# Softmax sums of couples 7 to 9 put in front of the next scores, in a fused attention and SiLU kernel on one core

## The chip, the cores and the metric

The kernel runs on one core of one Trainium2 chip. The metric is device time in microseconds (us) of one execution; the number that counts is the median of the runs. All data is float32 inside; inputs arrive as float64 where the reference makes them so (the weights `w_in` and `w_out`) and are rounded on the chip.

## The reference, cut to what matters

There are 8 batches of 12 heads, 448 rows and a head width of 64; the model width is 768, the hidden width 2048.

```python
q_n, k_n = rmsnorm(q, g_q), rmsnorm(k, g_k)          # each (8, 12, 448, 64)
scores = (1 / sqrt(64)) * q_n @ k_n.T
attn = exp(scores - max);  attn = attn / (sum(attn) + 1e-9)
x = (attn @ v) -> rows (8*448, 12*64)
h = x @ w_in                                          # (3584, 2048)
out = (h * sigmoid(h)) @ w_out                        # (3584, 768)
```

## The kernel before, in words

**Couples.** Four heads of one batch are a couple (two pairs of two heads). There are NC = 24 couples; GROUP = 6 couples make two batches, LATE is 9 and SOON is 11. The attention of the couples and the first matrix product (x @ w_in) of the two batches before run interleaved on TensorE: couple c is one `visit(c)` (scores, exponentials on ScalarE, weighted sums of v) followed by one `between(c)` in which TensorE is filled with products of x @ w_in. In the trace a visit of couple 8 or later begins with the two small matmuls of line 718 (the row factors of a later couple) and the first scores of line 752.

**The first product.** It is computed by a seven-product scheme in blocks m = 0 to 7 (`Seven`): the products are called "1" to "7" and run in the order 1, 2, 6, 5, 7, 3, 4. Each takes three matmuls of 128x448, recorded as six, into a PSUM bank of its own. The results of 1 and 5 are copied out by ScalarE (L974, L983), those of 2, 6, 7, 3 and 4 are added on VectorE (L912, `plus`); POOL adds two more terms from SBUF (L984, L987). Before "3" is taken out, POOL's L984 has to be done, and before "4", L987.

**PSUM banks.** Products take their bank alternately from two pools: `mm` with two buffers, and, in stretches, `sc` with two buffers, which the scores use as well. A buffer is free for its next user when the instruction that empties it is done. So in `mm` each product waits until the one two places earlier in `mm` has been taken out.

**Softmax sums.** `sum_up(c)` adds the exponentials over the keys by four matmuls with a block of ones (L832, tiles of 128x32, recorded as eight). Then VectorE takes reciprocals in two halves (L841), copies them (L847), and four small DMAs on SyncE's queue spread them over partitions (`spread`, L850). `divide` (L863) multiplies the weighted sums with them. For an ordinary couple L832 stands within the second half of `between(c)`, in a bank of `sc`, and `divide` reads the weighted sums of v from their PSUM banks in the next visit, with one operand in PSUM and one in SBUF. For couples in the list `LAGGED` (before: 10, 12 to 16, 18 to 22) L832 stands at the very end of `between(c)`, just in front of the next couple's scores, in a bank of `mm`; the two reciprocals run in the next visit (`lagging`), the weighted sums are copied to SBUF without division, and `divide` runs on SBUF data within the next `between`.

**Rounding w_in.** The 24 pieces of `w_in` are each loaded ahead by SyncE (L88), opened by two ScalarE instructions (L103, L104, step "o") and rounded by three VectorE instructions (L126, L129, L133) and one of POOL (L137, step "r"). `halves` says which steps run in which half of which `between` (two halves for each couple from GROUP on: entry 0 is couple 6's first half, entry 3 couple 7's second, 5 couple 8's second, 7 couple 9's second); `visits` says which run in a visit. A round issues the next load. `sum_w_in(i, step)` makes the four sums of chunk i of six pieces that products 6, 5, 7 and 3 use (steps 1, 0, 2 and 3; VectorE on 128x768, L912 and L909).

**The order of work.** The kernel writes the order out by hand: a piece of VectorE, ScalarE, POOL or SyncE work is emitted between matmuls at fixed shares of a `fill`, and each engine runs its queue in that order. Nothing is reordered at run time.

**Other lines named below.** L475 and L474 sum and square k rows; L503 and L722 raise to the power -1/2 on POOL; L731 scales q rows; L682 and L686 transpose q and k on VectorE, L692 applies the gains on ScalarE; L803 adds exponentials; L699 and L705 square and sum q; L643 and L674 are TensorE's transposes of earlier couples; L314, L325, L327, L255, L287 and L289 load v, q and k; L1002 saves hidden rows.

Of the kernel before, what the change touches and what calls it, by code (L numbers as in the profile page):

```python
# [542 lines left out]
def bounded(  # L543
# [10 lines left out]
    NC, loads, place, norm, spare, ones, first, squares = (  # L554
        own[name] for name in ("NC", "loads", "place", "norm", "spare", "ones", "first", "squares")
    )
    GROUP, LATE = z.NPAIR, z.LATE
    EARLY = GROUP - 1
    SOON = 2 * GROUP - 1
    FULL = (GROUP, SOON - 1)  # L560
    LAGGED = [c for c in range(SOON - 1, NC) if c % GROUP != GROUP - 1]


    hidden = dram.tile([z.NF, P, z.B * S], F32, name="hidden")
# [6 lines left out]
    work = mem.tile([P, 16 * S + z.NK], F32, name="work")  # L571
# [11 lines left out]
    r = [piece(S) for _ in range(2)]  # L583
# [10 lines left out]
    late = [extra[:, ds(2 * z.NW * S - (i + 1) * n, n)].bitcast(I32) for i in range(2)]  # L594
# [71 lines left out]
    def transpose_k(c):  # L666


        assert z.KB == BANK
        t = ps.tile([P, 2, BANK], F32, name="sc", bufs=2)  # L670
        rows = place[f"k{c % 2}"]
        for i in range(2):
            for j in range(z.KEYS + 1 - i):
                nc.tensor.transpose(t[:, i, ts(j, P)], rows[:, ds((z.KA, z.KB)[i] + j * P, P)], ident)  # L674
        columns = t.rearrange("p i s -> p (i s)")[:, 0 : z.NK]
        nc.scalar.activation(kT, columns, AF.Copy, scale=gains)
        loads["k" if c < LATE - 1 else "quarters"](min(c + 2, LATE))

    def flip(c, name):

        if name == "q":
            nc.vector.transpose(qT.rearrange("p i s -> p (i s)"), q_of(c)[:, 0 : z.NK])  # L682
            if c > SOON:
                load_q(c + 1)
            return
        nc.vector.transpose(kT, place[z.BY_QUARTERS])  # L686
        if c + 1 < NC:
            loads["quarters"](c + 1)
# [171 lines left out]
    def divide(c, source):  # L860
        for i in range(2):
            x = x_of(c, i)
            nc.vector.tensor_tensor(  # L863
                out=x, in0=x if source is None else source[i], in1=factors(c)[i], op=ALU.mult
            )
# [155 lines left out]
    def sum_w_in(i, step):  # L1021

        assert room.w_in.rounded >= (i + 1) * z.NW
        summed.add((i, step))
        w = room.chunk(i).rearrange("p (c m r k) -> p c m r k", c=z.NW, m=2, r=2)
        up, low = w[:, 0:HW], w[:, HW:]
        s = room.sums(i).rearrange("p (s c m k) -> p s c m k", s=3, c=HW, m=2)
        left_sums(
            up[:, :, :, 0], low[:, :, :, 0], up[:, :, :, 1], low[:, :, :, 1],
            s[:, 0], s[:, 1], s[:, 2], (step,),  # L1030
        )
# [165 lines left out]
    for at in ((1, 2), (2, 1), (2, 2)):  # L1197
        a = take(2 * z.HALF)
        results[at] = [a[:, ts(t, z.HALF)] for t in range(2)]
    a = take(2 * z.HALF)  # L1200
# [251 lines left out]


    step_of = {"o": lambda: room.w_in.open(), "r": lambda: room.w_in.round()}
    halves = {0: "ro", 1: "ro", 2: "ro", 3: "oro", 4: "or", 5: "oor", 6: "o", 7: "oroo"}
    visits = {GROUP + 2: "rr", GROUP + 3: "r", GROUP + 4: "rr"}
    for c in range(GROUP // 2):
        halves[2 * (c - GROUP)], halves[2 * (c - GROUP) + 1] = "rr", "o"
    halves[-2], halves[-1] = "r", ""
# [3 lines left out]
    sums_visits = {GROUP + 1: 1, GROUP + 3: 2}  # L1463
# [4 lines left out]
        return work + [lambda a=a: sum_w_in(*a) for a in sums_halves.get(i, ())]  # L1468

    def weights_in_visit(c):  # L1470
        for step in visits.get(c, "")[1:]:
            step_of[step]()
        rows = [lambda: scale_rows(c + 1, nc.vector)] if LATE - 1 <= c < SOON else []
        if c in sums_visits:
            sum_w_in(sums_visits[c], 0)
        run_all(rows)
        if c in sums_visits:
            for step in range(1, 4):
                sum_w_in(sums_visits[c], step)

    def last_two(c):
# [2 lines left out]
    def visit(c):  # L1484

        beside = normalise(c + 1) if 0 < c <= GROUP else []
        if c == GROUP:
            beside = [lambda: None] + beside[2:]
        if c < NC:
            scores(c, 0, 0)  # L1490
        for step in visits.get(c, "")[:1]:
            step_of[step]()
        if lagging:
            lagging.pop(0)()
        if c == 0:
            first_q(1)
            normalise_alone(1)
            scores(c, 1, 0)
        if c == 0:
            run_all(beside[0:1])  # L1500
        else:
            weigh(c - 1, LEFT)
            weigh(c - 1, LEFT - 1, 0)
            turn(1, nc.scalar.copy if c <= GROUP else nc.vector.tensor_copy)
            run_all(beside[0:1])
            if GROUP < c < NC and c % GROUP == 0:
                sum_x(last_two(c), 0, range(2, 4))
        if c < NC:
            scores(c, 0, 1)
        if c > 0:  # L1510
            weigh(c - 1, LEFT - 1, 1)
            if c - 1 < EARLY:
                for i in range(2):
                    nc.vector.tensor_copy(x_of(c - 1, i), sums[i])  # L1514
                run_all(beside[1:2])
                if c == GROUP // 2 + 1:
                    divide(c - 2, None)
                if inverting:
                    while len(inverting) > 1:
                        inverting.pop(0)()  # L1520
                    if c > 1:
                        divide(c - 2, None)
            else:
                if lagging:
                    for i in range(2):
                        nc.vector.tensor_copy(x_of(c - 1, i), sums[i])
                    lagging.pop(0)()
                else:
                    divide(c - 1, sums)
                if c == GROUP:  # L1530
                    for i in range(1, HW):
                        sum_x(last_two(c), i, range(2))
                    for i in range(2):
                        norm.scale(c + 1, q_of(c + 1), q_of(c + 1), i, nc.vector)
                    room.w_in.round()
                run_all(beside[1:2])
                if GROUP < c < NC and c % GROUP == 0:
                    for i in range(1, HW):
                        sum_x(last_two(c), i)
                weights_in_visit(c)  # L1540
            if c + 1 < NC:
                loads["vrest"](c + 1)
        if c == NC:
            return
        if c > 0:
            scores(c, 1, 0)
        scores(c, 1, 1)
        if c <= GROUP:
            run_all(beside[2:3])
        weigh(c, 0, 1)  # L1550
        scores(c, 2, 0)
        weigh(c, 1, 1)
        turn(0, nc.scalar.copy)
        if c < GROUP:
            run_all(beside[3:4])
        scores(c, 2, 1)
        weigh(c, 0, 0)
        if c < GROUP:
            scores(c, LEFT)
        if c != GROUP - 1:  # L1560
            run_all(add(c, 1))
        weigh(c, 1, 0)
        if c < GROUP // 2:
            room.w_in.open()
        if c >= GROUP:
            scores(c, LEFT)
        if c + 1 < NC:
            loads["v"](c + 1)
        if len(inverting) == 1:
            inverting.pop()()  # L1570
# [5 lines left out]
    def between(c):  # L1576

        def transposes_and_sums():
            if c in LAGGED:
                first = [lambda: divide(c - 1, None)] if c - 1 in LAGGED else [lambda: None]  # L1580
                return first + [lambda: None, lambda: flip(c + 1, "k"), gain]
            summing = sum_up(c)
            if c < GROUP - 1:
                transpose_k(c + 1)
            if c < GROUP:
                next(summing)
            if c == GROUP - 1:
                reciprocals = next(summing)
                divide(c - 1, None)
                sum_x([0, 1], 0)  # L1590
                run_all(reciprocals)
                return
            if GROUP <= c < LATE - 1:
                transpose_k(c + 1)
            reciprocals = next(summing)
            if LATE - 1 <= c < NC - 1:
                reciprocals += [lambda: flip(c + 1, "k"), gain]
            if GROUP // 2 < c < EARLY:
                divide(c - 1, None)
            return reciprocals  # L1600
# [23 lines left out]
        late = add(c, LEFT - 1) if c >= GROUP else []  # L1624
# [4 lines left out]
        if c == GROUP:  # L1629
            third, fourth = (  # L1630
                [lambda i=i, step=step: sum_x(last_two(c), i, (step,)) for i in range(1, HW)]
                for step in (2, 3)
            )
            late = third + late + fourth
        late += further[2:] if c >= GROUP else further[:2]
        if c - 1 in LAGGED and c not in LAGGED:
            late.append(lambda: divide(c - 1, None))
# [284 lines left out]
```

## Time and profile before

| | us |
|---|---|
| median of 3 runs | 1294.24 |
| lowest and highest | 1294.24 and 1294.8 |
| profiled execution | 1296.34 |
| its span, first to last instruction | 1294.6 |
| TensorE busy in the span | 1283.5 |
| VectorE busy | 971.4 |
| ScalarE busy | 504.3 |
| POOL busy | 363.5 |

The profiled execution is one run by itself, with 1.74 us outside its span, and stands 2.1 us above the median. The granted TensorE clock is 0.999 over the span. All starts in the lines of the trace are microseconds from the span's start; a line gives start, length, engine, source line, operation, output and inputs, and how many instructions were merged; a bracket tells idle time ahead of it and what ended it. Lengths of successive instructions overlap by some 0.05 to 0.1 us, so queues are best summed from start to start.

In this trace the visits of couples 7, 8, 9, 10 and 11 begin at 147.09, 180.44, 212.35, 244.27 and 276.77 us.

### The profile page before, as it was taken

How to read it: one execution, taken by the hardware profiler on the slowest of the kernel's cores; microseconds unless marked ns; L12 is line 12 of the kernel's file. 1: busy time of each engine (PE TensorE's matmuls, PEld its weight loads, DVE VectorE, ACT ScalarE, POOL GpSimd, SP SyncE). 2: the span in 40 equal slices, each digit the busy share in tenths (PEclk: the TensorE clock that was granted, in tenths of full speed). 3: DMA queues.
4: the chain of work that ended last, by engine and by line, in shares of the span. 5: the costliest groups of instructions: out<-in, count | busy, mean ns of one | idle time of the engine just before them, and what ended most of it. 6: DMA issues, size and time to landing. Idle time of an engine off the chain costs nothing.

```text
span 1294.6 us, 19931 instructions
## 1 busy us (share of the span) xinstructions
PE 1283.5 (99%) x7212; PEld 840.7 (65%) x7212; DVE 971.4 (75%) x1672; ACT 504.3 (39%) x880; POOL 363.5 (28%) x221
## 2 busy tenths in 40 slices
PE   9999999999999999999999999999999999999998
PEld 4444454444444454444544555559999999999998
DVE  6898878868666558666555886798978787878785
ACT  7967666645555554554543344310001000000000
POOL 6765454543344344343311344400000000000000
PEclk9999999999999999999999999999999999999999
DMA  9675347434444444444411466312332313141411
GB/s 232 174 193 136 104 124 197 95 83 102 112 94 91 119 91 102 108 93 93 107 50 69 149 204 219 117 66 88 100 94 86 113 67 129 51 133 48 141 39 40
DMA packets 266160, 144.15 MB, mean 111 GB/s; under 512 B 203748, under 2 KB 249956, under 8 KB 266052
## 3 DMA queue, kind: packets, MB, share of 16 engines
q1 hardware_dynamic: 265424, 141.68, 39.8%
q8 instruction: 59, 0.97, 0.3%
q0 software_dynamic: 320, 0.90, 0.2%
q14 instruction: 49, 0.40, 0.1%
q10 hardware_dynamic: 308, 0.20, 0.1%
HBM read 95.36 MB, written 41.29 MB: 106 GB/s over the span
## 4 chain that ended last, share of the span: by engine, by line
PE 97%; DVE 1%; POOL 1%; issue 0%; ACT 0%; DMA 0%; SPq 0%; ACTq 0%; DVEq 0%; POOLq 0%
PE alone L1285 23%; PE mm L963 21%; PE sc L963 11%; PE av L789 10%; PE sc L752 10%; PE mm L1285 8%; PE alone L963 7%; PE alone L1323 2%; PE mm L832 2%; PE mm L1323 1%; PE sc L643 1%; PE sc L832 1%; PE sc L674 0%; DVE work L912 0%; POOL rms L503 0%
## 5 line engine op out<-in xcount | busy, mean ns | idle before, releaser
L757 ACT ACTIVATE work<-sc,rms 128x448 f32<-128x448 f32 x318 | 182.0, 635 | 98.0 <-PE sc L752 85.7
L752 PE MATMUL sc<-work 64*64 64x448 f32 x1344 | 169.4, 543 | 1.0 <-ACT work L653 0.6
L789 PE MATMUL av<-work,rows 64*64 64x448 f32 x1272 | 155.5, 540 | 1.2 <-DVE x L1514 0.9
L963 PE MATMUL mm<-x,W 128*128 128x448 f32 x366 | 149.1, 542 | 0.0
L963 PE MATMUL mm<-sums_x,W 128*128 128x448 f32 x348 | 142.4, 542 | 0.0
L803 DVE TENSOR_TENSOR work<-work 128x896 f32<-128x896 f32 (+1 forms) x110 | 118.3, 1105 | 28.6 <-PE av L789 28.1
L530 POOL DMA_DIRECT2D out_dram<-x x2 | 1.2, 592 | 443.5 <-DVE x L912 443.5
L503 POOL TENSOR_TENSOR rms<-rms,minus_half 128x14 f32<-128x14 f32 (+4 forms) x40 | 97.4, 2437 | 86.8 <-DVE rms L499 83.3
L963 PEld LDWEIGHTS mm<-x,W 128*128 128x128 f32 x366 | 68.5, 190 | 70.3 <-issue 64.8
L1285 PE MATMUL alone<-W,rows 128*128 128x192 f32 x610 | 113.0, 326 | 0.0
L963 PEld LDWEIGHTS mm<-sums_x,W 128*128 128x128 f32 x348 | 65.1, 190 | 68.1 <-issue 62.5
L789 PEld LDWEIGHTS av<-work,rows 64*64 64x64 f32 x1272 | 65.9, 132 | 62.8 <-issue 19.3
L752 PEld LDWEIGHTS sc<-work 64*64 64x64 f32 x1344 | 60.4, 132 | 63.3 <-ACT work L757 25.3
L1285 PEld LDWEIGHTS alone<-W,rows 128*128 128x128 f32 x610 | 101.4, 190 | 0.0
L963 PE MATMUL sc<-x,W 128*128 128x448 f32 x246 | 99.6, 541 | 0.0
L984 POOL TENSOR_TENSOR stage<-parts,stage 128x448 f32<-128x448 f32 x31 | 39.8, 1285 | 169.2 <-ACT stage L983 168.9
L722 POOL TENSOR_TENSOR rms<-rms,minus_half 128x28 f32<-128x28 f32 x15 | 72.6, 4842 | 48.9 <-DVE rms L719 47.8
L963 PEld LDWEIGHTS sc<-x,W 128*128 128x128 f32 x246 | 46.4, 190 | 47.0 <-issue 46.7
L1285 PE MATMUL alone<-W,work 128*128 128x192 f32 x382 | 72.2, 326 | 0.0
L1295 ACT COPY rows<-alone 128x192 f32<-128x192 f32 x33 | 10.5, 318 | 141.5 <-PE alone L1285 136.7
L1285 PEld LDWEIGHTS alone<-W,work 128*128 128x128 f32 x382 | 63.8, 190 | 0.0
L1116 ACT ACTIVATE stage<-stage 128x896 f32<-128x896 f32 x63 | 56.8, 945 | 17.1 <-DVE stage L912 16.9
(267 smaller groups left out, 2312.8 us busy)
## 6 DMA issues: line engine op xcount, KB each, us to landing
hidden<-stage SPq DMA_DIRECT2D x63, 448.0 KB, 2.9
work<-hidden SPq DMA_DIRECT2D x21, 1024.0 KB, 5.1
rows<-in_moe_w_out_dram SPq DMA_DIRECT2D x32, 384.0 KB, 3.7
W<-in_moe_w_in_dram SPq DMA_DIRECT2D x22, 512.0 KB, 5.3
x<-hidden SPq DMA_DIRECT2D x7, 1024.0 KB, 6.1
rows<-in_q_dram SPq DMA_DIRECT2D x120, 56.0 KB, 2.2
rows<-in_k_dram SPq DMA_DIRECT2D x120, 56.0 KB, 2.3
rows<-in_k_dram SPq DMA_DIRECT2D x60, 96.0 KB, 2.6
```

Of the source, the lines that this page charges most:

```text
L503: nc.gpsimd.tensor_tensor(out=t, in0=t, in1=half, op=ALU.pow)
L722: nc.gpsimd.tensor_tensor(out=f, in0=f, in1=minus_half.to_broadcast([P, n]), op=ALU.pow)
L752: nc.tensor.matmul(two[ds(half * D, D), h, 0:S], keys[rows, ts(half, D)], qT[rows, pair, :], start=True, stop=True,)
L757: nc.scalar.activation(left_weights(c)[:, h] if j == LEFT else weights(c, j)[:, i, h], two[:, h, 0:S], AF.Exp, scale=norm.column(c, i, h, j),)
L789: nc.tensor.matmul(sums[i][ds(h * D, D), :], v, w, start=(j == 0 and step == 1), stop=(j == LEFT - 1 and step == 1),)
L803: nc.vector.tensor_tensor(out=total, in0=total, in1=more, op=ALU.add)
L832: nc.tensor.matmul(t[ds(h * D + i * n, n), :], ones[:, which + i if which else 0], left_weights(c)[:, h] if which else w()[:, i, h], start ...
L963: nc.tensor.matmul(t, self.left(name, s), self.right(name, s), start=s == ends[0], stop=s == ends[1])
L984: nc.gpsimd.tensor_tensor(out=done[1, 2], in0=u2, in1=p5, op=ALU.add)
L1116: nc.scalar.activation(t, t, AF.Silu)
L1285: nc.tensor.matmul(t, x[:, i], y, start=i == ORDER[0], stop=i == ORDER[-1])
L1323: nc.tensor.matmul(o, a[:, 2 * i + m, t], right_one(name, i)[:, m], start=n == 0, stop=n == len(steps) - 1,)
```

## The change

Couples 7, 8 and 9 join `LAGGED`: their L832 goes to the end of `between`, into a bank of `mm`, their reciprocals and spreading DMAs into the next visit, their division onto SBUF data in the half after that. Three roundings leave the visits of couples 8, 9 and 10 and run at the end of the second halves of couples 7, 8 and 9. The roundings that stay in the visits of couples 8 and 10 keep their place. The last two of the four sums of chunk 2 of `w_in` leave the visit of couple 9 and become the first VectorE work of couple 9's first half.

```diff
-    LAGGED = [c for c in range(SOON - 1, NC) if c % GROUP != GROUP - 1]
+    LAGGED = [c for c in range(GROUP + 1, NC) if c % GROUP != GROUP - 1]
...
-    halves = {0: "ro", 1: "ro", 2: "ro", 3: "oro", 4: "or", 5: "oor", 6: "o", 7: "oroo"}
-    visits = {GROUP + 2: "rr", GROUP + 3: "r", GROUP + 4: "rr"}
+    halves = {0: "ro", 1: "ro", 2: "ro", 3: "oror", 4: "or", 5: "oorr", 6: "o", 7: "oroor"}
+    visits = {GROUP + 2: "r", GROUP + 4: "r"}
...
     def weights_in_visit(c):
-        for step in visits.get(c, "")[1:]:
+        for step in visits.get(c, ""):
             step_of[step]()
...
-            for step in range(1, 4):
+            for step in range(1, 2 if c - 1 in LAGGED else 4):
                 sum_w_in(sums_visits[c], step)
...
             scores(c, 0, 0)
-        for step in visits.get(c, "")[:1]:
-            step_of[step]()
         if lagging:
             lagging.pop(0)()
...
             if c in LAGGED:
-                first = [lambda: divide(c - 1, None)] if c - 1 in LAGGED else [lambda: None]
-                return first + [lambda: None, lambda: flip(c + 1, "k"), gain]
+                work = [lambda: divide(c - 1, None) if c - 1 in LAGGED else None, lambda: None]
+                if c < LATE - 1:
+                    transpose_k(c + 1)
+                    return work
+                return work + [lambda: flip(c + 1, "k"), gain]
...
+        if c in sums_visits and c - 1 in LAGGED:
+            late = [lambda a=a: sum_w_in(sums_visits[c], a) for a in (2, 3)] + late
```

## The prediction

> **What bounds the kernel now.** I read the page first: the busy shares of the engines and the chain that ended last.
>
> ```profile
> PE 1283.5 (99%) x7212; PEld 840.7 (65%) x7212; DVE 971.4 (75%) x1672; ACT 504.3 (39%) x880; POOL 363.5 (28%) x221
> ...
> PE 97%; DVE 1%; POOL 1%; issue 0%; ACT 0%; DMA 0%; SPq 0%; ACTq 0%; DVEq 0%; POOLq 0%
> ```
>
> TensorE is the chain, and in a span of 1294.6 us it lacks 11.1 us of being always busy. The change takes no matmul away. It can gain only from seams between matmuls, and lose only where TensorE comes to wait. So the second view is TensorE's timeline, around L832 in couple 9 (within the products) and in couple 14 (already in front of the scores).
>
> ```profile
> 232.55 0.92 PE L963 MATMUL mm<-sums_x,W 128*128 128x448 f32 x2
> 233.39 0.96 PE L832 MATMUL sc<-work,ones 128*32 128x448 f32 x8
> 234.28 1.77 PE L963 MATMUL mm<-sums_x,W 128*128 128x448 f32 x4
> 235.89 2.42 PE L963 MATMUL sc<-x,W 128*128 128x448 f32 x6
> 238.14 2.42 PE L963 MATMUL mm<-x,W 128*128 128x448 f32 x6
> 240.40 3.92 PE L963 MATMUL mm<-sums_x,W 128*128 128x448 f32 x10
> 244.25 0.24 PE L718 MATMUL sc<-rms,ident 64*64 64x28 f32 x2
> ...
> 405.28 2.42 PE L963 MATMUL mm<-sums_x,W 128*128 128x448 f32 x6
> 407.63 0.96 PE L832 MATMUL mm<-work,ones 128*32 128x448 f32 x8
> 408.52 0.24 PE L718 MATMUL sc<-rms,ident 64*64 64x28 f32 x2
> ```
>
> See the starts, not the lengths. Two products take 240.40 - 235.89 = 4.51 us, so a record takes 0.376 and a product 2.255. The eight records of L832 run four at a time, 0.75 together. The third view is the end of couple 7's `between` on POOL and VectorE:
>
> ```profile
> 174.43 1.50 POOL L737 COPY ident<-ident 32x32 f32<-32x32 f32 x4
> 176.01 1.57 POOL L984 TENSOR_TENSOR stage<-parts,stage 128x448 f32<-128x448 f32 x1
> 177.55 1.28 POOL L137 TENSOR_TENSOR W<-W 128x512 int32<-128x512 int32 x1
> 178.79 1.12 POOL L987 TENSOR_TENSOR stage<-parts,stage 128x448 f32<-128x448 f32 x1
> ```
>
> ```profile
> 178.03 0.61 DVE L912 TENSOR_TENSOR stage<-mm,stage 128x448 f32<-128x448 f32 x1
> 179.95 0.62 DVE L912 TENSOR_TENSOR stage<-mm,parts 128x448 f32<-128x448 f32 x1 [1.30 <-POOL stage L987]
> ```
>
> The last line takes product "4" out of its `mm` bank. It waited 1.30 us for POOL's L987, because "4" is written over the copy of "5" that L987 reads. Nobody on TensorE needed that bank before the next visit, so the wait was free.
>
> **The seams (gain).** Within the products, 232.55 to 235.89 is 3.34 us for 6 records and one L832, 8 x 0.376 = 3.01 of work: 0.33 of seam. In front of the scores, 405.28 to 408.52 is 3.24 for the same work: 0.23, and this holds the step to L718 that couple 9 pays separately (244.25 - 240.40 - 10 x 0.376 = 0.09). The move saves 0.33 + 0.09 - 0.23 = 0.19 us a couple, 0.58 for three.
>
> **Couple 7: L832 gets a new wait (loss).** In the new queue order L832 takes the `mm` bank of "4" of block 2; "3" and the first step of the next "1" stand between. So it now waits for the line at 179.95. When would TensorE be there? Its transposes L674 end and L832 follows at 169.56 in the old order; without the 0.09 seam the first product starts at 169.47, four products take 9.02, two records 0.75, the seam 0.09: 179.33. When is "4" out? VectorE has 3.3 us less ahead of it (171.66 to 174.97, the reciprocals and their copy, leave) and a round of 1.5 more (171.66 to 173.2, next L705 to 174.2, "7" out to 174.75, second round to 176.3), so it is ready early. POOL isn't: L503 and L737 keep their places (up to 176.0), then L984, L137, L987. L984 takes 1.13 to 1.14 elsewhere and 1.57 here; I take 1.3. With 1.24 from L137 to L987, 1.12 and 0.04 to VectorE and 0.6 for L912, "4" is out at 180.3. The wait is about 0.95 us; 0.74 if L984 takes 1.1, 1.24 if nothing on POOL moves. Behind L832 stand the row factors and all scores of couple 8, so the wait counts in full. POOL's extra L137 stands behind L987 and delays L722 by 0.2; L731, its user, has over 2 us.
>
> **Couple 8: no wait.** L832 takes the bank of "1" of block 4, which ScalarE copies out (L974). TensorE is there at 211.25 (191.51, two thirds of a product with its seam to 193.12, eight products). ScalarE's L692 needs the k transposition (L686). VectorE: in the visit the reciprocal takes the slot of the removed round, the copies L1524 cost what L863 cost from PSUM (row 184.59, two in 1.07), reciprocal and copy add 2.0 up to 187.7, the round that stays runs to 189.2 (its L129, 1.40 in the row at 186.11 under POOL's L137, is back at 0.43 as that L137 ran before), L731 to 190.2: the adds L803 begin at 190.25, before at 190.18. In the halves, reciprocals leave, a division of 1.1 and a round of 1.5 come: L686 ends near 207.9 (before 208.8), L692 at 209.1, L974 at 209.7. SyncE sends the four spreading DMAs (2.5 us) ahead of the v loads, and the chain of loads behind, L88 too, moves by 0.3 to 0.8. The open at 206.90, which waits for such a load, may slip so far; the round behind it, then L705, ends at 211 to 211.9, and the row factors need it at 212.1. So 0, and up to 0.3.
>
> **Couple 9: the tight queue.** VectorE has almost no idle time here. In the visit it is ahead: W sum, L731 (1.05, not the 2.19 of before, which overlapped a POOL L137 that is gone) and second W sum end at 222.4, 0.7 before the old start of the adds (223.16). From there in new order: two adds 2.0, q transposition 1.0, W sum 0.9, "6" out 0.55, W sum 0.9, three adds 3.0 (230.8), "7" out 0.55, add 1.05, "3" out when TensorE ends it (232.8 to 233.35), then two reductions around a ScalarE square 1.8, L499 0.1, division 1.1, "4" out 0.5, round 1.5, k transposition 1.0, round 1.5, "2" out 0.55: 241.4. The next "5" takes that bank, and TensorE is there at 232.55 + 4 x 2.255 = 241.57. Then L705 1.0 and "6" out 0.6 give 243.0; L832 wants the bank at 241.57 + 4 x 0.376 + 0.09 = 243.16. Both meet with 0.15 to spare: I take 0.1 lost, and bounds of 0 and 1.0 (a twentieth of a 20 us queue). Product "7" reads W after the moved sum (226.5 against 228.04), "3" after the other (227.9 against 230.29).
>
> **Couples 10 and 11** get the last division (1.1) and no other load; VectorE waited 1.89 and 2.07 us there at the end of couple 10's `between`. Zero.
>
> **Divisions in SBUF.** The row for a division on SBUF data beside POOL's power is 300.29 (two L863 in 1.17 us, with L503 running from 300.53): no price on VectorE; L503 took 2.82 instead of 2.59. I take zero.
>
> The Trainium skill speaks against it ("SBUF — State Buffer", section "Who interferes with whom"): an instruction of VectorE with two SBUF inputs shares its second read port with a POOL instruction that reads SBUF, and whoever comes second may stand; the old division, with one input in PSUM, did not. By the rule with POOL first, each couple could lose the 2.59 of a L503 on VectorE, enough to break couple 9; by the row VectorE issues first, right behind L499, and POOL pays.
>
> **Sum.** 0.95 - 0.58 + 0.1 = +0.47 us. The profiled execution's 1296.34 (span 1294.6 and 1.74 around it) stands 2.1 above the median, a difference between executions; the change is counted from the median: 1294.24 + 0.47 = 1294.7. A measurement of this kernel can tell about 0.2% (2.6 us) from no change, and this is far below.
>
> **Rivals.** *Only the seams move:* POOL does L984 and L987 sooner, or the bank of "4" is not the one waited for, and couple 9 holds. -0.58: 1293.7. For it: VectorE's inputs to L987 come 3 us sooner. Against: POOL's own queue, back to back from 174.43, doesn't depend on them.
>
> *Couple 9's queue breaks (slower):* one mechanism, VectorE's operations in couple 9 stretched by POOL. Rows: a W sum takes 0.95, or 1.89 at 260.19; L129 0.43 or 1.40; L731 1.08 or 2.19. Two sums (0.94 more each), two L129 (0.97 each) and one L731 (1.11) stretched make 1.88 + 1.94 + 1.11 = 4.9, minus 0.15 of slack: 4.8 us more on TensorE, 1294.7 + 4.7 = 1299.4. Beyond 0.2% it needs a wait of 2.2 there, half of these five. Against: the POOL work that stretched the rows (L137) leaves the visit.
>
> *Faster by over 0.2%:* would need 2.6 us; the three seams hold 1.0 in all. I see no way.
>
> **How the numbers follow.** Forecast (couple 7 waits, couple 9 about holds) 0.58; only the seams 0.28; couple 9 breaks 0.12; something unseen that gains 0.02. The range reaches down to the seams alone (1293.7, less the 0.2 between runs) and up over the upper bounds of the three couples (1.24 + 0.3 + 1.0 - 0.58 = 1.96, 1296.2, with 0.2 between runs): 1293.5 to 1296.4. That leaves out the broken queue and little else. Same takes 0.58 + 0.28 = 0.86, slower 0.12, faster 0.02.
>
> **What would show it.** In the new profile: L832 at the end of couple 7's `between` starts about 1 us after the last product record ends, right after the L912 that follows POOL's L987; couple 8's L832 follows without a gap; in couple 9 the last "5" and L832 start within 0.2 us of their places; the `between` stretches of couples 7, 8, 9 take about +0.75, -0.2 and -0.1 us. The reasoning is wrong if couple 7 shows no gap, if TensorE waits in couple 10 or later, or if the visits (11.07 us each) grow.

## The result, and the profile after

The changed kernel takes 1297.06 us (median of 19 runs, 1296.39 to 1299.13); the kernel before took 1294.8 in the runs beside it (19 runs, 1294.24 to 1295.96). The ratio is 1.0018, with a 95% interval of 1.0011 to 1.0026: slower by 2.3 us. This is within the 0.2% that the prediction called no change, but it is clear of zero, and it lies above the predicted range (1293.5 to 1296.4). Of the 0.66 us above it, 0.56 is the base: the range was counted from 1294.24, and the kernel before took 1294.8 here.

The profiled execution took 1297.79 us, its span 1296.0. Its page, engines and chain:

```profile
PE 1284.8 (99%) x7212; PEld 842.5 (65%) x7212; DVE 975.0 (75%) x1678; ACT 504.5 (39%) x880; POOL 362.0 (28%) x221
...
PE 80%; DVE 3%; DMA 1%; ACT 1%; SPq 1%; issue 0%; ACTq 0%; DVEq 0%
```

The 80% doesn't compare with the 97% of before: the shares add up to 86%, because the chain can be followed back only to 191.33 us. What it does show is that from there to 243.13 us it runs over VectorE, ScalarE and DMA and not over TensorE. TensorE's waits from 150 to 260 us (engine, line, whom it waited for: total, times, longest) name the place. Before, the same question had an empty answer.

```profile
PE mm L963 <- DVE stage L912: 2.1, 3, 0.7
```

Three waits, and TensorE's timeline puts one into the `between` of each of couples 7, 8 and 9:

```profile
175.26 2.42 PE L963 MATMUL mm<-sums_x,W 128*128 128x448 f32 x6
178.42 1.02 PE L963 MATMUL mm<-x,W 128*128 128x448 f32 x2 [0.74 <-DVE stage L912]
179.53 0.96 PE L832 MATMUL mm<-work,ones 128*32 128x448 f32 x8
180.42 0.24 PE L718 MATMUL sc<-rms,ident 64*64 64x28 f32 x2
...
206.65 2.42 PE L963 MATMUL mm<-x,W 128*128 128x448 f32 x6
209.75 2.52 PE L963 MATMUL mm<-x,W 128*128 128x448 f32 x6 [0.68 <-DVE stage L912]
212.20 0.96 PE L832 MATMUL mm<-work,ones 128*32 128x448 f32 x8
...
240.07 2.42 PE L963 MATMUL mm<-sums_x,W 128*128 128x448 f32 x6
243.13 1.77 PE L963 MATMUL mm<-sums_x,W 128*128 128x448 f32 x4 [0.65 <-DVE stage L912]
244.84 0.96 PE L832 MATMUL mm<-work,ones 128*32 128x448 f32 x8
```

From start to start, the six records at 175.26, 206.65 and 240.07 should take 2.255 us; the next product comes after 3.16, 3.10 and 3.06. So each wait costs 0.81 to 0.90 us. The restart behind it costs 0.10 more: two records span 1.02 us at 178.42, and 0.92 where nothing was waited for. Each of the three is a product that cannot have its `mm` bank, not L832. Why VectorE was late is in its own queue (couple 7 first, then 8, then 9), beside POOL's:

```profile
174.91 1.24 DVE L129 TENSOR_SCALAR W<-W 128x512 int32<-128x512 int32 x1
176.18 1.66 DVE L133 SCALAR_TENSOR_TENSOR W<-W 128x512 int32<-128x512 int32 x1
177.76 0.61 DVE L912 TENSOR_TENSOR stage<-mm,stage 128x448 f32<-128x448 f32 x1
...
190.19 3.09 DVE L803 TENSOR_TENSOR work<-work 128x896 f32<-128x896 f32 x2
...
206.50 1.67 DVE L133 SCALAR_TENSOR_TENSOR W<-W 128x512 int32<-128x512 int32 x1
208.09 1.10 DVE L686 STREAM_TRANSPOSE work<-rows 128x896 f32<-128x896 f32 x1
209.12 0.58 DVE L912 TENSOR_TENSOR stage<-mm,parts 128x448 f32<-128x448 f32 x1
...
228.23 4.03 DVE L803 TENSOR_TENSOR work<-work 128x896 f32<-128x896 f32 x3
...
240.59 0.76 DVE L126 TENSOR_SCALAR W<-W 128x512 f32<-128x512 f32 x1
...
242.46 0.62 DVE L912 TENSOR_TENSOR stage<-mm,stage 128x448 f32<-128x448 f32 x1
```

```profile
174.59 1.27 POOL L984 TENSOR_TENSOR stage<-parts,stage 128x448 f32<-128x448 f32 x1
175.82 1.46 POOL L137 TENSOR_TENSOR W<-W 128x512 int32<-128x512 int32 x1
...
189.30 2.02 POOL L137 TENSOR_TENSOR W<-W 128x512 int32<-128x512 int32 x1 [3.44 <-DVE W L133]
...
206.47 1.14 POOL L987 TENSOR_TENSOR stage<-parts,stage 128x448 f32<-128x448 f32 x1
...
229.60 1.72 POOL L984 TENSOR_TENSOR stage<-parts,stage 128x448 f32<-128x448 f32 x1 [11.10 <-ACT stage L983]
...
239.78 1.28 POOL L137 TENSOR_TENSOR W<-W,x 128x512 int32<-128x512 int32 x1 [0.29 <-DVE W L133]
```

Two rows of VectorE in the profile of before, for comparison:

```profile
175.90 0.69 DVE L133 SCALAR_TENSOR_TENSOR W<-W 128x512 int32<-128x512 int32 x1
...
190.18 2.16 DVE L803 TENSOR_TENSOR work<-work 128x896 f32<-128x896 f32 x2 [0.94 <-PE av L789]
```

Compare lengths: L129 takes 1.24 instead of 0.43, L133 1.66 and 1.67 instead of 0.69, two L803 3.09 instead of 2.16, three L803 4.03 where three of 1.05 would take about 3.1, and L126 0.76 instead of 0.42. Call such a row stretched. Each stretched row lies beside a POOL instruction of the second list. The L912 behind it is the line that empties the bank: "3" of couple 7's block at 177.76, "4" at 209.12, "2" at 242.46.

The stages that the change touches, from start to start in each profiled execution (us; "b7" is couple 7's `between` from its first product on, "v8" couple 8's visit):

| kernel | b7 | v8 | b8 | v9 | b9 | v10 | sum | against before |
|---|---|---|---|---|---|---|---|---|
| before | 21.52 | 11.07 | 20.85 | 11.07 | 20.85 | 11.07 | 96.43 | |
| changed | 22.50 | 11.07 | 21.60 | 11.07 | 21.57 | 11.07 | 98.88 | +2.45 |
| e1 lag only | 21.70 | 11.61 | 20.65 | 11.59 | 20.65 | 11.59 | 97.79 | +1.36 |
| e2 rounds only | 24.05 | 12.43 | 22.04 | 11.04 | 22.52 | 11.07 | 103.15 | +6.72 |
| e3 rounds behind | 21.71 | 11.06 | 20.65 | 11.06 | 20.65 | 11.06 | 96.19 | -0.24 |
| e4 no POOL | 21.42 | 11.07 | 20.65 | 11.07 | 20.74 | 11.07 | 96.02 | -0.41 |
| e5 from couple 8 | 21.52 | 11.07 | 20.65 | 11.06 | 20.65 | 11.06 | 96.01 | -0.42 |
| e6 round early | 21.53 | 11.06 | 20.65 | 11.06 | 20.65 | 11.06 | 96.01 | -0.42 |
| e7 sums in visit | 22.51 | 11.06 | 21.45 | 11.06 | 21.58 | 11.06 | 98.72 | +2.29 |
| e8 no L137 | 22.15 | 11.07 | 21.32 | 11.07 | 21.19 | 11.07 | 97.87 | +1.44 |

The last column of the changed kernel, +2.45, is the measured +2.26 within the spread of the runs. From couple 10's `between` on, its stages have the lengths of before. Each stage is from one execution: e7, whose program differs from the changed kernel only in couple 9, has 21.45 for couple 8 against 21.60, so a stage with a wait is good to some 0.15.

### The profile page after: what moved, and what is told of

Its sections match the earlier page's. It is cut to its first block, busy times and chain, and to the rows that moved or that the text cites. A ratio compares the mean times of both kernels' runs of the same rounds, so it can differ in the third digit from the quotient of the medians.

```text
span 1296.0 us, 19941 instructions
## 1 busy us (share of the span) xinstructions
PE 1284.8 (99%) x7212; PEld 842.5 (65%) x7212; DVE 975.0 (75%) x1678; ACT 504.5 (39%) x880; POOL 362.0 (28%) x221
## 4 chain that ended last, share of the span: by engine, by line
PE 80%; DVE 3%; DMA 1%; ACT 1%; SPq 1%; issue 0%; ACTq 0%; DVEq 0%
PE alone L1285 23%; PE mm L963 16%; PE sc L963 9%; PE mm L1285 8%; PE alone L963 7%; PE av L789 6%; PE sc L752 6%; PE alone L1323 2%; PE mm L832 1%; PE mm L1323 1%; DVE work L803 1%; DMA hidden<-stage 0%; DVE work L912 0%; SPq L255 0%; DMA x<-in_moe_w_in_dram 0%
## 5 line engine op out<-in xcount | busy, mean ns | idle before, releaser
L803 DVE TENSOR_TENSOR work<-work 128x896 f32<-128x896 f32 (+1 forms) x110 | 121.1, 1131 | 26.9 <-PE av L789 26.4
L503 POOL TENSOR_TENSOR rms<-rms,minus_half 128x14 f32<-128x14 f32 (+4 forms) x40 | 98.0, 2452 | 82.5 <-DVE rms L499 78.0
L984 POOL TENSOR_TENSOR stage<-parts,stage 128x448 f32<-128x448 f32 x31 | 38.6, 1246 | 170.5 <-ACT stage L983 170.2
L722 POOL TENSOR_TENSOR rms<-rms,minus_half 128x28 f32<-128x28 f32 x15 | 71.9, 4796 | 48.0 <-DVE rms L719 45.7
```

The costliest lines, as they stand in the source:

```text
L503: nc.gpsimd.tensor_tensor(out=t, in0=t, in1=half, op=ALU.pow)
L722: nc.gpsimd.tensor_tensor(out=f, in0=f, in1=minus_half.to_broadcast([P, n]), op=ALU.pow)
L803: nc.vector.tensor_tensor(out=total, in0=total, in1=more, op=ALU.add)
L984: nc.gpsimd.tensor_tensor(out=done[1, 2], in0=u2, in1=p5, op=ALU.add)
```

## The experiments

Each was timed in 5 rounds beside the kernel before. The first four ran on one chip with a before of 1294.43 us, the other four with 1294.18.

**e1: only the lag.** LAGGED grows, with the order of a lagged couple's work that belongs to it; roundings and W sums stay.

```diff
-    LAGGED = [c for c in range(SOON - 1, NC) if c % GROUP != GROUP - 1]
+    LAGGED = [c for c in range(GROUP + 1, NC) if c % GROUP != GROUP - 1]
```

> Only the list LAGGED grows by couples 7 to 9; the roundings and the W sums stay where they were before. Theory A (the roundings moved into the halves, together with what POOL stretches, make VectorE late with a product's bank): the three `between` stretches of couples 7 to 9 lose their seam and nothing else, about -0.2 us each against before (21.5, 20.85, 20.85), no TensorE wait on L912 there; but in the visits of couples 8, 9 and 10 a round now stands ahead of the reciprocal and of L765, so each visit grows by 0.5 to 0.9 us; in all +1 to +2 us. Rival B (the bank of `mm` that L832 now takes is what TensorE waits for, the prediction's step for couple 7): couple 7's `between` still grows by 0.5 to 1 us without the roundings. Rival C (the divisions on SBUF data cost VectorE): couples 8 and 9 still wait.

1296.12 us, ratio 1.0014 (1.0005 to 1.0023). Couples 8 and 9 lose exactly the seam (20.65), the three visits grow by 0.52 to 0.54 each, and couple 7 grows by 0.18. TensorE's waits:

```profile
PE av L789 <- DVE av L765: 0.9, 3, 0.3
PE mm L832 <- DVE stage L912: 0.3, 1, 0.3
```

The first line is the round that now stands ahead of L765 in each of three visits; where they stay, the lag costs 0.5 us in each visit. The second is the prediction's own step for couple 7: L832 waits for product "4", but 0.3 us (0.38 from start to start) and not 0.95. Divisions on SBUF data (rival C) cost couples 8 and 9 nothing.

**e2: only the rounds.** The `halves` and `visits` of the change, LAGGED and sums as before.

```diff
-    halves = {..., 3: "oro", 4: "or", 5: "oor", 6: "o", 7: "oroo"}
-    visits = {GROUP + 2: "rr", GROUP + 3: "r", GROUP + 4: "rr"}
+    halves = {..., 3: "oror", 4: "or", 5: "oorr", 6: "o", 7: "oroor"}
+    visits = {GROUP + 2: "r", GROUP + 4: "r"}
```

> Only the three roundings move from the visits to the halves; LAGGED and the W sums as before. Theory A: VectorE has the 1.5 us of each round and the reciprocals in the same half, so TensorE waits for L912 in couples 7 to 9 as much as in the changed kernel or more: 0.7 us or more each, +2 us or more in all. Rival B: no wait, since L832 is in its old bank of `sc`: the time of before within 0.3 us.

1299.86 us, ratio 1.0043 (1.0031 to 1.0055). With L832 in its old bank the waits are there and larger (the longest 2.0 us):

```profile
PE mm L963 <- DVE stage L912: 4.2, 3, 2.0
```

So the roundings make the waits, and the bank of L832 doesn't. The reciprocals, which here are still in the halves, make them worse: in couple 8 neither the round nor the adds are stretched (L133 0.69, two adds 2.09), and TensorE waits 0.93 all the same. The stages of this profile say +6.7 us, the median of the runs +5.4. And 1.36 us of the stages are in couple 8's visit (12.43), where TensorE waits for nobody:

```profile
179.53 1.30 PE L963 MATMUL mm<-x,W 128*128 128x448 f32 x2 [1.98 <-DVE stage L912]
```

Behind this wait two records span 1.30 us instead of 1.02. The granted clock is 0.76 from 179.5 to 180.7 us, 0.50 from 180.7 to 183.5, and 0.99 after that: the longest wait is paid a second time, at half the clock. In the changed kernel, whose waits are 0.9 at most, the clock stays at 1.00 behind couple 7's wait.

**e3: the three rounds behind the half.** The changed kernel, with each moved round emitted after the last product of its half.

```diff
-    halves = {..., 3: "oror", 4: "or", 5: "oorr", 6: "o", 7: "oroor"}
+    halves = {..., 3: "oro", 4: "or", 5: "oor", 6: "o", 7: "oroo"}
+    behind = (GROUP + 1, GROUP + 2, GROUP + 3)
...
+        if c in behind:
+            step_of["r"]()
         if c % GROUP == GROUP - 1:
```

> The changed kernel, but the three moved roundings run behind the last product of the half, where VectorE had 1.3, 0.5 and 1.5 us idle ahead of L719. Theory A: the waits of couples 8 and 9 go (about -0.85 us each), couple 7 keeps a wait of 0.2 to 0.9 us for product 4, which hangs on POOL's L987; in all -0.6 to +0.5 us against before. Rival B: couple 7 keeps its full 1.2 us. Rival C: couples 8 and 9 keep 0.85 us each; then +2 us as in the changed kernel.

1294.29 us, ratio 0.9996 (0.9988 to 1.0005). Couples 8 and 9 no longer wait, the visits stay at 11.06, and couple 7 keeps one wait, in front of L832:

```profile
176.81 0.92 PE L963 MATMUL mm<-x,W 128*128 128x448 f32 x2
178.04 0.96 PE L832 MATMUL mm<-work,ones 128*32 128x448 f32 x8 [0.31 <-DVE stage L912]
```

```profile
177.36 0.62 DVE L912 TENSOR_TENSOR stage<-mm,parts 128x448 f32<-128x448 f32 x1 [1.71 <-POOL stage L987]
```

This is product "4" behind POOL's L987, the link that the prediction drew. From 176.81 to 178.04 are 1.23 us; two records and the switch need 0.84, so it costs 0.38. The adds of couples 8 and 9 are as stretched here as in the changed kernel (couple 8's two take 3.15; couple 9's three follow), and yet nobody waits:

```profile
225.78 4.03 DVE L803 TENSOR_TENSOR work<-work 128x896 f32<-128x896 f32 x3
```

So stretched adds without the round in the half do no harm.

**e4: without POOL beside the rounds.** From couple 7's `between` to couple 10's visit POOL's L137, L984 and L987 are left out.

```diff
-            nc.gpsimd.tensor_tensor(out=wi, in0=wi, in1=low, op=ALU.add)
+            if not QUIET["on"]:
+                nc.gpsimd.tensor_tensor(out=wi, in0=wi, in1=low, op=ALU.add)
...
+        QUIET.update(on=GROUP < c < SOON - 1)
```

> The changed kernel without three kinds of POOL instruction from couple 7's `between` to couple 10's visit: L137 (the low bits of some pieces of w_in) and L984 and L987 (two terms of the first product) are left out there, so this part of the result is not the reference's. Theory A with stretching: the rows that grew on VectorE (L129 1.24, L133 1.66 and 1.67, L803 by 0.9 to 1) fall back to 0.43, 0.69 and 1.05, and the waits of all three couples go: -0.6 us against before. Rival D (the queue is too long even without POOL): the waits stay at 0.5 us or more in couples 8 and 9.

1294.19 us, ratio 0.9999 (0.9990 to 1.0008). The rounds are where the change puts them, and the rows have their short lengths again (the lines of this kernel are numbered 2 to 3 higher: L131 is L129, L135 is L133, L806 is L803):

```profile
174.12 0.43 DVE L131 TENSOR_SCALAR W<-W 128x512 int32<-128x512 int32 x1
174.58 0.69 DVE L135 SCALAR_TENSOR_TENSOR W<-W 128x512 int32<-128x512 int32 x1
...
225.45 3.08 DVE L806 TENSOR_TENSOR work<-work 128x896 f32<-128x896 f32 x3
```

The waits are gone but for 0.09 us in couple 9 and 0.10 in couple 7 (20.74 and 21.42, where 20.65 and 21.32 would be a seam saved and nothing lost). So the queue without stretching is just short enough, as the prediction's sum had it. With e3 this says that in the changed kernel neither the rounds nor the stretching makes the waits alone; both together do. For couple 7 this run has a second reading, as "3" and "4" no longer wait for POOL's sums either.

**e8: only L137 left out.** As e4, with L984 and L987 kept.

> The changed kernel without POOL's L137 (the low bits of some pieces of w_in, left out) from couple 7's `between` to couple 10's visit; L984 and L987 stay. It tells apart which POOL instruction stretches which row. Theory A by overlap in the changed kernel's trace: couple 7's L133 (1.66 beside L137) falls to 0.7 and its waits go or fall below 0.3; couple 8's L803 (beside L137) falls by 0.9, its L133 (beside L987) stays at 1.67, and the wait falls from 0.85 to 0 to 0.5; couple 9's L803 (beside L984) stays stretched and its wait stays at 0.5 to 1 us. If couple 9's wait goes too, L984 is not its cause.

1296.45 us, ratio 1.0019 (1.0009 to 1.0028); the stages say +1.44. Couple 8's pair of L803 is back at 2.09, its L133 stays at 1.66, and its wait falls from 0.85 to 0.57. Couple 9's three L803 still take 4.03 beside L984, and its wait falls from 0.81 to 0.43, since L126 is back at 0.39. For couple 7 the expectation failed: its L133 stays long, and its wait falls only from 0.90 to 0.72.

```profile
174.95 1.50 DVE L135 SCALAR_TENSOR_TENSOR W<-W 128x512 int32<-128x512 int32 x1
```

```profile
174.60 1.31 POOL L990 TENSOR_TENSOR stage<-parts,stage 128x448 f32<-128x448 f32 x1
```

With L137 away POOL's L987 (L990 here) moves up and meets the same instruction. L133 is 0.16 shorter than in the changed kernel, and the wait by about as much. Taking one POOL instruction out lets the next one in.

**e7: the two W sums back in the visit.** The changed kernel without its third part.

```diff
-            for step in range(1, 2 if c - 1 in LAGGED else 4):
+            for step in range(1, 4):
...
-        if c in sums_visits and c - 1 in LAGGED:
-            late = [lambda a=a: sum_w_in(sums_visits[c], a) for a in (2, 3)] + late
```

> The changed kernel with the two W sums of couple 9 back in its visit. Theory A (the round ahead of the k transposition and stretched adds make couple 9 late): VectorE has the same work ahead of product 2's bank, so couple 9 still waits 0.4 to 1 us, and the total is that of the changed kernel, +2 us, within 0.5. Rival E (the two moved sums are what makes couple 9 late): its wait goes, total +1.2 us.

1296.91 us, ratio 1.0021 (1.0012 to 1.0030): +2.7, a little over what was expected; the stages say +2.29. Couple 9's `between` is 21.58 against 21.57: the moved sums neither cost nor save (rival E falls).

**e5: no lag for couple 7.** As e3, but LAGGED begins at couple 8 and visit 8 keeps both rounds.

```diff
+    LAGGED = [c for c in range(GROUP + 2, NC) if c % GROUP != GROUP - 1]
+    behind = (GROUP + 2, GROUP + 3)
+    visits = {GROUP + 2: "rr", GROUP + 4: "r"}
```

> As the kernel with the rounds behind the half, but couple 7 is an ordinary couple again and visit 8 keeps both its rounds. Theory A: couple 7's `between` is that of before (21.5 us), couples 8 and 9 keep their -0.2 us each, the visits stay at 11.07: -0.4 us against before, the best so far by 0.2. Rival B: the same. If the gain of a seam is not there, it is the time of before.

**e6: one more round in couple 7's first half.** As e3, with `halves` 2: "ror", 3: "oo".

> As the kernel with the rounds behind the half, but one more round of couple 7 runs in its first half, so that POOL's L137 is out of the way of L987. Theory A: product 4 is out early enough and L832's last wait in couple 7 (0.3 to 0.4 us) goes: couple 7's `between` at 21.3, in all -0.6 us against before. Against it: if POOL's queue is late for another reason (L503, L737), the 0.4 stay.

e5 took 1294.97 us, ratio 1.0005 (0.9996 to 1.0014), e6 1294.17, ratio 1.0000 (0.9991 to 1.0009). Both have the stages that were expected for couples 8 and 9, and -0.42 us in sum. In e6 couple 7 does not gain: "4" waits no longer for POOL, but for TensorE's own end.

```profile
177.20 0.63 DVE L912 TENSOR_TENSOR stage<-mm,parts 128x448 f32<-128x448 f32 x1 [0.65 <-PE mm L963]
```

L832 comes two records after "4" ends, and taking "4" out needs 0.63 us: in this order couple 7's seam is lost (21.53), and the expected 21.3 was missed. No version here is faster than the kernel before by what the times can show. e5, with -0.42 in its stages, has a median 0.8 us above before. The 0.4 us are seen in the stages alone: the first 145 us, in front of the change, differ more. Couple 7's visit begins at 147.09 us in the profile of before, 146.12 in the changed kernel, 144.83 in e7 and 147.06 in e5, with the same order of instructions up to there.

## Why the prediction was wrong, point by point

- **The step that failed** is the sum of VectorE's queue: it priced the moved rounds at 1.5 us and the adds at 1.0 each, as they run alone. The runs showed moved rounds of 1.9 to 3.3 us and, in couples 8 and 9, an add that took a whole microsecond more beside POOL, and three waits of TensorE, of 0.81 to 0.90 us, for banks that this queue empties.
- **What bounds the kernel, and the seams: right.** TensorE loses its time in the waits, and a seam is worth 0.19 us predicted, 0.20 measured (20.85 to 20.65 in e1, e3, e5, e6).
- **Couple 7: the sum near by luck, the place wrong.** Predicted +0.76 through L832 waiting 0.95 for "4"; measured +0.98, of which 0.90 is the next "1" waiting for "3", and 0.16 L832. The step that failed is "so it is ready early": the second round was summed at 1.5 us and took 3.3 (174.45 to 177.76). It also began 0.67 later than summed, because L705 waited 0.61 for ScalarE's L699, which an opening (L103, L104) now precedes. Only "4" was timed; the bank of "3", which the next "1" needs, was not. The wait that was predicted is real, but 0.38 in e3: POOL's L737 took 0.99 there instead of 1.50 and L984 1.12 instead of 1.57. "L984 takes 1.13 to 1.14 elsewhere" was a misreading: in the profile of before it also takes 1.91 at 228.85 and 2.02 at 257.14.
- **Couple 8: wrong.** Predicted "no wait", -0.19 in all; measured +0.75. It looked at the bank that L832 takes; the wait came on the bank of "4", which the last product needs. By its own sum (L686 done at 207.9) "4" would be out at 208.4, with TensorE there at 208.9; it was out at 209.70. The adds at 190.19 took 0.9 more beside a later L137, of which all but 0.3 was made up in idle time before L863 at 203.43, and L133 took 1.0 more beside L987.
- **Couple 9: the term mis-sized.** Predicted 0.1 lost, upper bound 1.0; measured 0.81. It is the right bank ("2", for the next "5") and the right queue. The three adds took 1.0 more beside L984, of which 0.4 was left when "3" was out, and L126 nearly 0.4 more.
- **The rival "queue breaks": its mechanism was the right one.** VectorE stretched by POOL was named, with these rows and prices, but for couple 9 alone, as five stretched instructions or none. It came as two in each of three couples. It got a chance of 0.12, because "the POOL work that stretched the rows (L137) leaves the visit"; it left the visit for the half, where L984 and L987 also run, and one of its own rows (the W sum at 260.19, 1.89 us) lay beside L987 at 259.35, not beside L137.
- **The divisions: right.** Two L863 take 1.17 us beside POOL's L503, which takes 2.90 instead of 2.59. What the Trainium skill ("SBUF — State Buffer", "Who interferes with whom") says of two SBUF inputs beside POOL is what the adds and L133 show here, and so is the order that the prediction took from it (whoever comes second may stand; the last section has the rows). The prediction weighed it for the one instruction whose row spoke against it, and for no other that moved.
- **The range.** Its upper end summed 1.24, 0.3 and 1.0; the 0.3 of couple 8 was 0.94 (0.75 and the seam). Couples 7 and 9 stayed within theirs (1.17 and 0.91, with the seam).

What stays open: L129 and L126, which read only one tile of SBUF, are stretched too (1.24 and 0.76, beside L984 and L137). The runs show that they are, and not why.

## What to carry to other kernels

When instructions move on a queue, price them by what they will lie beside, not by the row at their old place: sum the queue once with short and once with long rows, and if the slack at a PSUM bank is smaller than one stretch, count a wait. Work whose result is not needed soon goes behind the last instruction that empties a bank, where the engine idles: three rounds moved by a few places took the 2.4 us back. A tuned order can hold several parts that need each other: here, by the stages, the lag alone costs 1.4 us, the rounds alone 6.7, the whole change 2.4.

## What the runs showed of the hardware

Not every POOL instruction stretches VectorE. L722, the power, runs 5.1 us, and a round inside it kept its short lengths (VectorE and POOL in the profile of before):

```profile
245.15 0.43 DVE L129 TENSOR_SCALAR W<-W 128x512 int32<-128x512 int32 x1
245.61 0.69 DVE L133 SCALAR_TENSOR_TENSOR W<-W 128x512 int32<-128x512 int32 x1
```

```profile
244.87 5.11 POOL L722 TENSOR_TENSOR rms<-rms,minus_half 128x28 f32<-128x28 f32 x1 [2.70 <-DVE rms L719]
```

L722 itself is longer here, 5.11 where it takes 4.80 at 181.06 in the changed kernel; L126 was already running (244.70 to 245.12) when it began.

With the additions L137, L984 and L987 over 448 and 512 columns, the one that begins second is stretched, whichever engine it is on. In couple 9 of the changed kernel an add of VectorE begins 0.05 us ahead of L987 and keeps its length, and L987 takes 2.03 instead of 1.14:

```profile
232.83 1.09 DVE L803 TENSOR_TENSOR work<-work 64x896 f32<-64x896 f32 x1
```

```profile
232.88 2.03 POOL L987 TENSOR_TENSOR stage<-parts,stage 128x448 f32<-128x448 f32 x1 [1.56 <-DVE parts L912]
```

In couple 8 L987 begins 0.03 ahead of L133 (206.47 and 206.50); L987 keeps 1.14, and L133 takes 1.67. In the profile of before couple 7's L133 (175.90, 0.69) was ahead of L984 (176.01, 1.57) by 0.11, and POOL paid. The second is longer by a little less than what is left of the first: L126 at 240.59 by 0.34, with 0.47 left of L137; L133 at 206.50 by 0.98, with 1.11 left of L987. So a sum of a queue beside POOL needs the starts and not only the lengths, and a shift of a few hundredths of a microsecond decides which engine pays.

And TensorE pays for a wait twice: after each one the first record is followed by the next after 0.48 us instead of 0.376. After the 2.0 us of e2 it ran at half the granted clock for some 3 us more.
